# Four heads to a transfer: one decode step of attention and MLP with its reads regrouped into 64-KB rows

## The chip, the core and the metric

The kernel runs on one NeuronCore of a Trainium2 chip. The metric is device time in microseconds (us) from the start to the end of one execution. A NeuronCore has a matrix engine (TensorE, "PE" in the profile, its weight loads "PEld"), VectorE ("DVE"), ScalarE ("ACT"), GpSimd ("POOL") and SyncE ("SP"), which here only issues transfers. Each engine runs its own instructions in order and waits for others by semaphores. Sixteen DMA engines bring data from device memory (HBM) into the on-chip memory SBUF, which has 128 partitions. PE writes its results into PSUM, a smaller memory with 128 partitions and eight banks of 512 fp32 columns.

## What is computed

One token for each of two batch entries goes through attention over a cache of 4,096 keys and values in 32 heads of 128, and through an MLP; a sigmoid gate mixes the two. Everything is fp32. Cut to what matters:

```python
B, Sq, D = 2, 1, 576
H, Sk, Dh = 32, 4096, 128
F = 4608

def _A_ref(x, k_cache, v_cache, wq, wo):
    B, Sq, D = x.shape
    H, Dh = 32, 128
    q = (lambda x, *d: x.transpose(*d))((x @ wq).reshape(B, Sq, H, Dh), 0, 2, 1, 3)
    scores = jnp.einsum("bhqd,bhkd->bhqk", q, k_cache) * (Dh ** -0.5)
    p = _softmax(scores, axis=-1)
    o = jnp.einsum("bhqk,bhkd->bhqd", p, v_cache)
    return (lambda x, *d: x.transpose(*d))(o, 0, 2, 1, 3).reshape(B, Sq, H * Dh) @ wo

def _B_ref(x, w1, b1, w2, b2):
    h = jnp.einsum("bsd,df->bsf", x, w1) + b1
    h = _gelu(h)
    return jnp.einsum("bsf,fd->bsd", h, w2) + b2

x = A_x
g = _sigmoid((x * gate_w).sum(-1, keepdims=True))
a = _A_ref(x, A_k_cache, A_v_cache, A_wq, A_wo)
b = _B_ref(x, B_w1, B_b1, B_w2, B_b2)
return g * a + (1 - g) * b
```

K and V hold 134.2 MB each; wq and wo 9.4 MB each, w1 and w2 10.6 MB each. Each byte is used once for the one token of its batch entry (the weights once for both).

## The kernel before

The unit of work is one head of one batch entry, 64 units in all. A unit's K is 4,096 rows of 128 numbers, 2 MB. `load_head` (L94) brings it in with one transfer, 32 consecutive rows to a partition, so that each partition receives one run of 16 KB; V the same way. Weights come in by `load_w` (L83: wq and w1 in pieces of 128 rows, 16 or 18 KB to a partition, and a last piece of 64 rows cut in two halves), `load_w2` (L100: eight pieces, 11.5 or 9.2 KB to a partition, the last one cut further) and `load_wo` (L139: sixteen pieces, two runs of 2.3 KB to a partition).

**Order of the transfers.** All large transfers are issued by SP. A list (`seq`, L114 to 121) fixes the order: wq, w1, K0, K1, then V(i) and K(i+2) in turn, then w2. They share nine buffers of 18 KB to a partition (`SLOTS`, L59), taken in rotation; a transfer waits until the last reader of its buffer is done. wo has two buffers of its own and is issued at every fourth unit, between the others. x, the gate's weights, b1 (as 512 runs of 36 bytes) and b2 are issued by ACT at the start (L147 to 150). The order of the instructions on every engine is the order of the program (`manual_schedule`, L75).

**Start.** x is transposed on PE (L181), the gate is computed (L188 to 196), `proj` (L199) multiplies x with wq: four column groups of PE work side by side, each with 32 columns of weights (x for both batch entries and zeros) and 512 columns of wq. The result, one row of q per batch entry and quarter, is copied to `qrow`. `q_unit` (L224) spreads four heads' q over all 128 partitions with one more matmul and a copy by ScalarE (L232), since VectorE needs q on every partition. Then b2 goes into the accumulator `acc` (L253) and `proj` multiplies x with w1. `mlp_t` (L270) transposes the MLP's hidden row in 36 pieces, three at each of twelve units, and `mlp_gelu` (L276) makes the activations.

**A unit**, in four stages that lie one pass of the loop (L368) apart:

- scores: VectorE multiplies K in place with q, first 12 of the 32 rows of each partition (`mul_a`, L300), then 20 (`mul_b`, L307). The sums over 128 numbers: the first 12 rows by ScalarE, one activation with an accumulator for each (L302), the other 20 by one VectorE reduction (L311); then the largest score of each partition (L315);
- softmax: PE transposes the 128 maxima (L319), VectorE takes the largest (L323), PE spreads it (L325), ScalarE takes the exponentials and their sums (L331);
- AV: eight matmuls per unit, each with four rows of V to a partition (512 columns), in four column groups in turn (L338), and a copy by ScalarE (L346). In the trace each fp32 matmul is two matmul instructions, each with its weight load;
- `combine` and `norm`: five matmuls pick the useful parts out of the AV result and add them over the partitions (L352, L355); VectorE divides by the sum (L360, L363). After every second unit `wo_mm` multiplies the head's result for both batch entries with its 128 rows of wo into `acc` (L246).

**End.** When the last unit is done, `mlp_out` (L288) multiplies the MLP's activations with w2 into `acc`; VectorE and ScalarE copy half of `acc` each (L415, L416), and SP and ACT write the result (L419).

Of the kernel before, what the change touches and what calls it, by code (L numbers as in the profile page):

```python
# [13 lines left out]

ACT_ROWS = 12
# [3 lines left out]
def kernel(  # L19
# [18 lines left out]
    N = B * H  # L38
    R = SK // P
    RB = 512 // DH  # L40
    NT = R // RB
    NX = D // P
    HALF = D - NX * P
    assert HALF * 2 == P
    NG = 4
    WQ = H * DH
    QG = WQ // NG
    HU = 512 // DH
    FG = F // NG
    FR = FG // P  # L50
    FB = 3
    FC = FG // FB
    NF = F // P
    HO = 2
    UO = HO * B
    NC = 4
    DO = D // NC
    SCALE = float(DH) ** -0.5
    SLOTS = 9  # L59
    W2A = 5  # L60
    PL = 120

    cp = ctx.enter_context(tc.tile_pool(name="cp", bufs=1))
    bp_ = ctx.enter_context(tc.tile_pool(name="bp_", bufs=SLOTS))
    wp2 = ctx.enter_context(tc.tile_pool(name="wp2", bufs=2))
    qp = ctx.enter_context(tc.tile_pool(name="qp", bufs=4))
    sp = ctx.enter_context(tc.tile_pool(name="sp", bufs=4))
    ep = ctx.enter_context(tc.tile_pool(name="ep", bufs=2))
    ps_acc = ctx.enter_context(tc.tile_pool(name="ps_acc", bufs=1, space=bass.MemoryType.PSUM))
    ps_av = ctx.enter_context(tc.tile_pool(name="ps_av", bufs=2, space=bass.MemoryType.PSUM))  # L70
    ps_big = ctx.enter_context(tc.tile_pool(name="ps_big", bufs=1, space=bass.MemoryType.PSUM))
    ps_sm = ctx.enter_context(tc.tile_pool(name="ps_sm", bufs=4, space=bass.MemoryType.PSUM))


    ctx.enter_context(tc.manual_schedule())  # L75


    kt, vt, wqt, wot, w1t, w2t = {}, {}, {}, {}, {}, {}

    def slot(name, n):  # L80
        return bp_.tile([P, FG * NG], F32, tag="slot", name=name)[:, :n]

    def load_w(w, c, name):  # L83

        n = w.shape[1]
        if c < NX:
            t = slot(f"{name}{c}", n)
            nc.sync.dma_start(t, w[c * P:(c + 1) * P])
        else:
            t = slot(f"{name}{c}", n // 2)  # L90
            nc.sync.dma_start(t, w[NX * P:].rearrange("q (e n) -> (q e) n", e=2))
        return t

    def load_head(src, i, name):  # L94

        t = slot(f"{name}{i}", R * DH)
        nc.sync.dma_start(t, src[i % B, i // B].rearrange("(p r) d -> p (r d)", p=P))
        return t.rearrange("p (r d) -> p r d", d=DH)

    def load_w2(g, part):  # L100
        lo, hi = (0, W2A) if part == 0 else (W2A, FR)
        t = slot(f"w2_{g}_{part}", (hi - lo) * D)
        src = w2[g * FG:(g + 1) * FG].rearrange("(p r) n -> p (r n)", r=FR)
        if (g, part) == (NG - 1, 1):

            m = hi - 1
            nc.sync.dma_start(t[:, :(m - lo) * D], src[:, lo * D:m * D])
            for a, z in ((0, PL), (PL, P)):
                nc.sync.dma_start(t[a:z, (m - lo) * D:], src[a:z, m * D:hi * D])
        else:  # L110
            nc.sync.dma_start(t, src[:, lo * D:hi * D])
        return t.rearrange("p (r n) -> p r n", n=D)

    seq = [("wq", c) for c in range(NX + 1)] + [("w1", c) for c in range(NX + 1)]  # L114
    seq += [("k", 0), ("k", 1)]
    for i in range(N):
        seq.append(("v", i))
        if i + 2 < N:
            seq.append(("k", i + 2))
    seq += [("w2", (g, part)) for g in range(NG) for part in range(2)]  # L120
    seq = seq[::-1]

    def load(n=1):
        for _ in range(n):
            if not seq:
                return
            kind, i = seq.pop()
            if kind == "wq":
                wqt[i] = load_w(wq, i, "wq")
            elif kind == "w1":  # L130
                w1t[i] = load_w(w1, i, "w1_")
            elif kind == "k":
                kt[i] = load_head(k_cache, i, "k")
            elif kind == "v":
                vt[i] = load_head(v_cache, i, "v")
            else:
                w2t[i] = load_w2(*i)

    def load_wo(g):  # L139
        t = wp2.tile([P, HO, D], F32, tag="wo", name=f"wo{g}")  # L140
        nc.sync.dma_start(t, wo[g * HO * P:(g + 1) * HO * P].rearrange("(c p) n -> p c n", p=P))
        return t

    xg = cp.tile([B + 1, D], F32, name="xg")
    b1T = cp.tile([P, NG, FR], F32, name="b1T")
    b2r = cp.tile([B, D], F32, tag="row", name="b2r")
    nc.scalar.dma_start(xg[:B], x.rearrange("b s d -> (b s) d"))  # L147
    nc.scalar.dma_start(xg[B:B + 1], gate_w[None, :])
    nc.scalar.dma_start(b1T, b1.rearrange("(g p r) -> p g r", p=P, r=FR))
    nc.scalar.dma_start(b2r[:1], b2[None, :])  # L150
    load(SLOTS)


    ident = cp.tile([P, P], F32, name="ident")
    make_identity(nc, ident)
    ones = cp.tile([P, P], F32, name="ones")
    nc.vector.memset(ones, 1.0)
    srow = cp.tile([1, P], F32, name="srow")
    nc.vector.memset(srow, SCALE)
    NPB = 4  # L160
    pt = []
    for j in range(NPB):
        t = cp.tile([P, 2 * R], F32, name=f"p{j}")
        nc.vector.memset(t, 0.0)
        pt.append(t)

    sel = cp.tile([P, RB], F32, name="sel")
    nc.vector.tensor_copy(sel, ident[:, 0:RB])
    for j in range(1, 4):
        nc.vector.tensor_add(sel, sel, ident[:, 32 * j:32 * j + RB])  # L170

    xe = cp.tile([B + 1, 2, P], F32, name="xe")
    nc.vector.memset(xe, 0.0)
    for e in range(2):
        nc.vector.tensor_copy(xe[:, e, e::2], xg[:, NX * P:])
    xps = ps_sm.tile([P, NX + 2, 4], F32, tag="sm", name="xps")
    for c in range(NX + 2):
        src = xg[:, c * P:(c + 1) * P] if c < NX else xe[:, c - NX]  # L180
        nc.tensor.transpose(xps[:, c, :B + 1], src, ident[:B + 1, :B + 1])  # L181
    xT = cp.tile([P, NX + 2, 32], F32, name="xT")
    nc.vector.memset(xT, 0.0)
    nc.vector.tensor_copy(xT[:, :, :B], xps[:, :, :B])
    gT = cp.tile([P, NX + 2], F32, name="gT")
    nc.vector.tensor_copy(gT, xps[:, :, B])

    zps = ps_sm.tile([P, B], F32, tag="sm", name="zps")  # L188
    for c in range(NX + 1):
        nc.tensor.matmul(zps, gT[:, c:c + 1].to_broadcast([P, P]), xT[:, c, :B], start=(c == 0), stop=(c == NX))  # L190
    gb = cp.tile([P, B], F32, name="gb")
    g1 = cp.tile([P, B], F32, name="g1")
# [6 lines left out]
    def proj(c, t, banks, width):  # L199
        for m, ps in enumerate(banks):  # L200
            for j in range(NG):
                o = (j * len(banks) + m) * width
                lhs = xT[:, c]
                if c == NX:
                    half = NG * len(banks) * width // 2
                    lhs = xT[:, NX + o // half]
                    o %= half
                nc.tensor.matmul(
                    ps[32 * j:32 * j + 32, :width], lhs, t[:, o:o + width], start=(c == 0), stop=(c == NX),
                    skip_group_check=True,  # L210
                )
# [24 lines left out]
    for b in range(B):  # L236
        q_unit(0, b)
# [210 lines left out]
```

## Time and profile before

| | |
|---|---|
| median of 3 runs | 743.46 us (743.27 to 743.82) |
| span of the profiled execution | 742.0 us, so that 1.5 us of the median lies around the span |
| DMA, mean over the span | 417 GB/s, 309.10 MB in 26,121 packets |
| PE, PEld | 470.7 and 228.8 us busy |
| DVE | 513.7 us busy |
| ACT | 311.7 us busy |
| mean granted clock of PE | 0.636 of full speed |

How to read it. The profile is one execution, recorded by the hardware. Its first part gives each engine's busy time, the second cuts the span into 40 equal slices (a digit is a busy share in tenths, "DMA" the mean share of the sixteen DMA engines, GB/s what they moved). The third lists the DMA queues: q1 is SP's, q10 is ACT's, q8 and q14 carry the engines' own instructions; a packet is one contiguous run moved by one engine. The chain of waits is followed back from the last instruction: at each step to what released it. In the groups by line, "x64" is a count, then come busy time and the mean duration of one in nanoseconds, then the idle time of the engine just before, with what ended it. The table of windows lists for a stretch its length, the busy time and count of PE, PEld, DVE, ACT and POOL, PE's granted clock, the DMA share and GB/s. In the timeline a row has start, duration, engine, line and operation, and in brackets the idle time before it. "SPq" is SP's instruction queue.

### The profile page before, as it was taken

The page shows a single profiled execution, that of the slowest core. Times are in us where ns is not written, and L with a number is a line of the kernel's source. Part 1 is how long each engine was busy: PE and PEld are TensorE (multiplying, and loading weights), DVE is VectorE, ACT ScalarE, POOL GpSimd, SP SyncE. Part 2 cuts the span into 40 slices and gives each one's busy share as a digit, 9 for nine tenths or more (in the row PEclk, how much of TensorE's full clock was granted, in tenths as well). Part 3 has the DMA queues.
Part 4 walks back from the last instruction along what each step waited for, and adds up shares of the span by engine and source line. Part 5 has one row for each costly group of instructions (what it writes and reads, how often), then busy time and mean ns, then how long its engine had stood idle before and what let it go on. Part 6 is the DMA issues. An engine that isn't in the chain of part 4 may idle for free.

```text
span 742.0 us, 8332 instructions
## 1 busy us (share of the span) xinstructions
PE 470.7 (63%) x2728; PEld 228.8 (31%) x2728; DVE 513.7 (69%) x477; ACT 311.7 (42%) x1817; POOL 0.7 (0%) x6
## 2 busy tenths in 40 slices
PE   4660869687766667667575665656555765566675
PEld 2110435354423323223231232222222333232343
DVE  1009869777887777886878867787778877777820
ACT  0104545444554445544445534454444544354410
POOL 0000000000000000000000000000000000000000
PEclk9985566657555655565656656666665665555568
DMA  9999999999999999999999999999999999999992
GB/s 368 427 427 423 429 424 430 422 430 423 426 427 427 423 430 425 425 426 427 426 426 427 424 427 425 428 427 426 427 426 428 424 427 425 429 422 428 424 422 108
DMA packets 26121, 309.10 MB, mean 417 GB/s; under 512 B 3155, under 2 KB 3163, under 8 KB 7519
## 3 DMA queue, kind: packets, MB, share of 16 engines
q1 hardware_dynamic: 25535, 308.56, 98.5%
q8 instruction: 21, 0.34, 0.2%
q14 instruction: 21, 0.17, 0.1%
q10 hardware_dynamic: 544, 0.03, 0.1%
HBM read 308.57 MB, written 0.00 MB: 416 GB/s over the span
## 4 chain that ended last, share of the span: by engine, by line
DMA 85%; PE 9%; DVE 5%; issue 0%; ACTq 0%; ACT 0%; DVEq 0%; SPq 0%
DMA k<-in_A_k_cache_dram 76%; PE av L338 8%; DMA w<-in_B_w_dram 6%; DVE k L300 4%; DMA b1T<-in_B_b_dram 3%; PE bp L325 1%; DVE nm L323 0%; DVE s L311 0%; DVE k L307 0%; PE acc L246 0%; PE op L352 0%; ACTq L147 0%; PE op L355 0%; PE mt L319 0%; DVE osb L415 0%
## 5 line engine op out<-in xcount | busy, mean ns | idle before, releaser
L302 ACT ACTIVATE k<-k 128x128 f32<-128x128 f32 x768 | 225.6, 295 | 297.6 <-DVE k L300 297.6
L300 DVE TENSOR_TENSOR k<-k,q 128x1536 f32<-128x1536 f32 x64 | 112.5, 1758 | 173.6 <-DMA k<-in_A_k_cache_dram 173.6
L338 PE MATMUL av<-v,p 128*32 128x512 f32 x1024 | 226.5, 1035 | 0.0
L311 DVE TENSOR_REDUCE s<-k 128x20 f32<-128x2560 f32 x64 | 179.8, 2810 | 0.1
L307 DVE TENSOR_TENSOR k<-k,q 128x2560 f32<-128x2560 f32 x64 | 179.4, 2803 | 0.0
L302 ACT ACTIVATION_READ_ACCUMULATOR k<-k 128x1 f32 x768 | 143.7, 187 | 0.0
L325 PE MATMUL bp<-nm,srow 1*128 1x1 f32 x128 | 36.9, 355 | 133.8 <-DVE nm L323 133.8
L352 PEld LDWEIGHTS op<-sel,avs 128*128 128x128 f32 x512 | 87.5, 258 | 3.7 <-issue 2.1
L352 PE MATMUL op<-sel,avs 128*128 128x1 f32 x512 | 84.7, 287 | 0.7 <-ACT avs L346 0.7
L319 PE MATMUL mt<-ident,m 128*1 128x128 f32 x64 | 20.4, 319 | 90.6 <-DVE m L315 90.1
L325 PEld LDWEIGHTS bp<-nm,srow 1*128 1x128 f32 x128 | 31.5, 304 | 139.4 <-DVE nm L323 137.5
L338 PEld LDWEIGHTS av<-v,p 128*32 128x32 f32 x1024 | 38.1, 159 | 84.2 <-issue 83.2
L319 PEld LDWEIGHTS mt<-ident,m 128*1 128x1 f32 x64 | 5.3, 83 | 143.1 <-DVE m L315 138.2
L346 ACT COPY avs<-av 128x512 f32<-128x512 f32 x64 | 37.4, 585 | 26.5 <-PE av L338 26.1
L355 PE MATMUL op<-rs,ones 128*128 128x1 f32 x128 | 31.2, 313 | 0.0
L355 PEld LDWEIGHTS op<-rs,ones 128*128 128x128 f32 x128 | 28.9, 278 | 0.0
L246 PE MATMUL acc<-wo,oT 128*2 128x144 f32 x256 | 18.4, 371 | 15.6 <-DMA wo<-in_A_wo_dram 15.0
L246 PEld LDWEIGHTS acc<-wo,oT 128*2 128x2 f32 x256 | 5.9, 91 | 61.7 <-issue 51.2
L227 PE MATMUL qb<-qrow,ident 128*128 128x512 f32 x32 | 23.6, 828 | 0.7 <-ACT q L232 0.7
L272 PEld LDWEIGHTS htp<-ident,hrow 128*128 128x128 f32 x72 | 18.5, 332 | 11.8 <-issue 11.6
L331 ACT ACTIVATE p<-s,bs 128x32 f32<-128x32 f32 x64 | 20.6, 321 | 2.1
L232 ACT COPY q<-qb 128x512 f32<-128x512 f32 x16 | 9.4, 585 | 26.6 <-PE qb L227 26.6
(57 smaller groups left out, 173.8 us busy)
## 6 DMA issues: line engine op xcount, KB each, us to landing
k<-in_A_k_cache_dram SPq DMA_DIRECT2D x64, 2048.0 KB, 35.1
v<-in_A_v_cache_dram SPq DMA_DIRECT2D x64, 2048.0 KB, 36.4
w<-in_B_w_dram SPq DMA_DIRECT2D x4, 2304.0 KB, 19.4
wo<-in_A_wo_dram SPq DMA_DIRECT2D x16, 576.0 KB, 36.4
wq<-in_A_wq_dram SPq DMA_DIRECT2D x4, 2048.0 KB, 14.7
w<-in_B_w_dram SPq DMA_DIRECT2D x4, 1440.0 KB, 37.0
w<-in_B_w_dram SPq DMA_DIRECT2D x4, 1152.0 KB, 26.0
wq<-in_A_wq_dram SPq DMA_DIRECT2D x1, 1024.0 KB
```

The costliest lines, as they stand in the source:

```text
L227: nc.tensor.matmul(ps, ident[:, 32 * j + b:32 * j + b + 1].to_broadcast([P, P]), qrow[:, m * 512:(m + 1) * 512], start=True, stop=True,)
L246: nc.tensor.matmul(acc[32 * s:32 * s + m], lhsT, rhs[:, s * DO:(s + 1) * DO], start=start, stop=stop, skip_group_check=True)
L300: nc.vector.tensor_mul(kt[i][:, :a], kt[i][:, :a], q.to_broadcast([P, a, DH]))
L302: nc.scalar.activation(kt[i][:, r], kt[i][:, r], AF.Copy, accum_out=st[i][:, r:r + 1])
L307: nc.vector.tensor_mul(kt[i][:, a:], kt[i][:, a:], q.to_broadcast([P, R - a, DH]))
L311: nc.vector.tensor_reduce(st[i][:, a:], kt[i][:, a:], AX.X, ALU.add)
L319: nc.tensor.transpose(mt[i], mx[i], ident)
L325: nc.tensor.matmul(bias[i], srow, nm, start=True, stop=True)
L338: nc.tensor.matmul(ps[32 * j:32 * j + 32], p[:, RB * t:RB * t + 32], vt[i][:, RB * t:RB * (t + 1)].rearrange("p r d -> p (r d)"), start=(t ...
L346: nc.scalar.copy(avs[i], ps)
L352: nc.tensor.matmul(ops[i][:, 0:1], avs[i][:, r * DH:(r + 1) * DH], sel[:, r:r + 1], start=(r == 0), stop=(r == RB - 1))
L355: nc.tensor.matmul(ops[i][:, 1:2], ones, rs[i], start=True, stop=True)
```

## The change

Nothing of what is computed changes. The unit is now a *quad*: four heads of one batch entry, 16 quads.

- **K and V.** `load_quad` reads the 8 MB of four heads with one transfer: 32 partitions to a head, 128 consecutive rows to a partition, one run of 64 KB each. Three slots of 64 KB to a partition take the place of the nine buffers: K alternates between slots 0 and 1, V has slot 2 alone (the last V goes to slot 0).
- **Order.** In pass i: scores of quad i; K(i+2) is issued, which waits for the sums over K(i) in the same slot; `combine` of quad i-1; AV of quad i; V(i+1) is issued, which waits for AV of quad i.
- **q.** The projection itself spreads q: for each batch entry and head its weights are one column of x, repeated 32 times, so that the result stands on the 32 partitions of that head. It stays in four PSUM banks, from where VectorE reads it. `q_unit` goes, and the scale is put into x (`xq`).
- **Scores.** VectorE alone multiplies and sums: one multiply and one reduction over all 128 rows of a partition. The maximum per 32 partitions is found by VectorE's 32 x 32 transpose, without PE. ScalarE takes four exponentials per quad, one for each head.
- **AV and combine.** 32 matmuls per quad. `combine` adds into one PSUM bank `oall` for all quads, four matmuls and one for the sums; division and transposition are done once at the end.
- **wq and w1** are read with four (or three) consecutive rows to a partition, 32 KB and 54 KB runs, into the slots that K and V take later. **w2 and wo** are read at the end, in runs of up to 63 KB, into slots that K and V have left: 28 of w2's 36 rows per partition after AV of quad 14, 28 of wo's 32 after the sums of quad 15, the rest after AV of quad 15. b1 is 128 runs of 144 bytes.
- **The MLP's** hidden row is transposed by VectorE (in slot 2) ahead of the first quad, and its product with b2 stands ahead of the q projection on PE. At the end two accumulators are added by PE, into whose bank the last four rows of wo go directly.

The new code, cut to its core:

```python
slots = [sb(f"slot{i}", P, SLOT) for i in range(3)]
...
    def load_quad(src, i, s):
        g, b = divmod(i, B)
        dma(slots[s], src[b, g * HQ:(g + 1) * HQ].rearrange("h (p r) d -> (h p) (r d)", p=HP))
...
    for u in range(2):
        nc.tensor.matmul(acc, g1z[:, u], b2r[:, u * DW:(u + 1) * DW], start=(u == 0), stop=False, skip_group_check=True)

    def q_mm(c, t, m, last):
        v = t.rearrange("p (g h d) -> p g h d", h=HQ, d=DH)
        for b in range(B):
            for h in range(HQ):
                nc.tensor.matmul(
                    qps[b][m][HP * h:HP * (h + 1)], xq[:, c, b:b + 1].to_broadcast([P, HP]), v[:, :, h],
                    start=(c == 0), stop=last, skip_group_check=True,
                )

    for c in range(NX):
        for m in range(2):
            o = c * WQ + m * WQ // 2
            q_mm(c, slots[0][:, o:o + WQ // 2], m, False)
    for e in range(2):
        q_mm(NX + e, wqh, e, True)
...
    def qk(i, s):
        g, b = divmod(i, B)
        k = slots[s].rearrange("p (r d) -> p r d", d=DH)
        q = qps[b][g // 4][:, (g % 4) * DH:(g % 4 + 1) * DH]
        nc.vector.tensor_mul(k, k, q.unsqueeze(1).to_broadcast([P, R, DH]))
        nc.vector.tensor_reduce(stt[i % 2], k, AX.X, ALU.add)
        nc.vector.tensor_reduce(mxt[i % 2], stt[i % 2], AX.X, ALU.max)
        nc.vector.transpose(mtt[i % 2], mxt[i % 2].to_broadcast([P, 32]))
        nc.vector.tensor_reduce(nmt[i % 2], mtt[i % 2], AX.X, ALU.max, negate=True)
        for h in range(HQ):
            a = slice(HP * h, HP * (h + 1))
            nc.scalar.activation(
                pt[i % 2][a, h:R * HQ:HQ], stt[i % 2][a], AF.Exp, bias=nmt[i % 2][a], accum_out=rst[i % 2][a]
            )

    def av(i, s):
        v = slots[s]
        for t in range(NT):
            j = t % 4
            nc.tensor.matmul(
                avp[i % 2][32 * j:32 * j + 32], pt[i % 2][:, 16 * t:16 * t + 32], v[:, 512 * t:512 * (t + 1)],
                start=(t < 4), stop=(t >= NT - 4),
            )
        nc.scalar.copy(avt[i % 2], avp[i % 2])
...
    def acc_row(name, r, last=False):
        lhs = (hg if name == "w2" else oT)[:, r]
        s = nset[0] % 2
        nset[0] += 1
        for u in range(2):
            nc.tensor.matmul(
                acc[64 * s + 32 * u:64 * s + 32 * u + B], lhs, wrow[name, r][:, u * DW:(u + 1) * DW],
                start=False, stop=last, skip_group_check=True,
            )

    load_quad(k_cache, 0, 0)
    load_quad(k_cache, 1, 1)
    load_quad(v_cache, 0, 2)
    N1 = NQ - 1
    for i in range(NQ):
        qk(i, i % 2)
        if i < NQ - 2:
            load_quad(k_cache, i + 2, i % 2)
        elif i == NQ - 2:
            load_quad(v_cache, N1, i % 2)
        else:
            load_rows("wo", 0, WA // 2, N1 % 2, 0)
            load_rows("wo", WA // 2, WA, N1 % 2, WA // 2)
        if i > 0:
            combine(i - 1)
        av(i, 2 if i < N1 else (NQ - 2) % 2)
        if i < NQ - 2:
            load_quad(v_cache, i + 1, 2)
        elif i == NQ - 2:
            load_rows("w2", 0, WA, 2, 0)
    load_rows("w2", WA, FR, 0, 0)
    load_rows("wo", WA, OR - 1, 0, FR - WA)
    load_rows("wo", OR - 1, OR, 0, FR - WA + OR - 1 - WA)
    combine(N1)
...
    for r in range(WA):
        acc_row("w2", r)
    for r in range(WA):
        acc_row("wo", r)
    for r in range(WA, FR):
        acc_row("w2", r, last=r >= FR - 2)
...
    accs = avt[1][:, :DW]
    nc.vector.tensor_copy(accs, acc)
    fin = qps[0][0][:, :DO]
    for v in range(4):
        nc.tensor.matmul(
            fin[32 * v:32 * v + B], fsel[:, v // 2], accs[:, (v % 2) * DO:(v % 2 + 1) * DO],
            start=True, stop=False, skip_group_check=True,
        )
    for r in range(WA, OR):
        for v in range(4):
            nc.tensor.matmul(
                fin[32 * v:32 * v + B], oT[:, r], wrow["wo", r][:, v * DO:(v + 1) * DO],
                start=False, stop=r == OR - 1, skip_group_check=True,
            )
```

(HQ is 4, HP 32, R 128, NT 32, NX 4, WA 28, FR 36, OR 32, DW 288, DO 144.)

More of the change, by code (lines that the diff above doesn't have):

```diff
@@ L13 @@
 P = 128
-ACT_ROWS = 12
 @with_exitstack
@@ L80, in slot @@
[L80 to L98, printed above, removed]
@@ L114 @@
[L114 to L137, printed above, removed]
@@ L139, in load_wo, with sb @@
[L139 to L146, printed above, removed]
+    pp = ctx.enter_context(tc.tile_pool(name="pp", bufs=1, space=bass.MemoryType.PSUM))
+    ctx.enter_context(tc.manual_schedule())
+    def sb(name, *shape):
+        return cp.tile(list(shape), F32, tag=name, name=name)
@@ L409 @@
[L409 to L416 removed]
+                oall[a, b * DH:(b + 1) * DH], sel[:, gp, rr], avt[i % 2][:, rr * DH:(rr + 1) * DH],
+                start=first and rr == 0, stop=last and rr == 3, skip_group_check=True,
+            )
+        nc.tensor.matmul(
+            oall[a, B * DH + b:B * DH + b + 1], hsel[:, gp], rst[i % 2], start=False, stop=last, skip_group_check=True
+        )
@@ L417 @@
+    osb = avt[0][:, :DO]
+    nc.vector.tensor_copy(osb, fin)
     for b in range(B):
```

395 lines of the change are left out of this document (157 added, 238 removed).

## The prediction

> **What bounds the kernel now.** I read the page first: busy shares, the forty slices, the queues and the chain.
>
> ```profile
> span 742.0 us, 8332 instructions
> PE 470.7 (63%) x2728; PEld 228.8 (31%) x2728; DVE 513.7 (69%) x477; ACT 311.7 (42%) x1817; POOL 0.7 (0%) x6
> DMA  9999999999999999999999999999999999999992
> GB/s 368 427 427 423 429 424 430 422 430 423 426 427 427 423 430 425 425 426 427 426 426 427 424 427 425 428 427 426 427 426 428 424 427 425 429 422 428 424 422 108
> q1 hardware_dynamic: 25535, 308.56, 98.5%
> q8 instruction: 21, 0.34, 0.2%
> q14 instruction: 21, 0.17, 0.1%
> q10 hardware_dynamic: 544, 0.03, 0.1%
> DMA 85%; PE 9%; DVE 5%; issue 0%; ACTq 0%; ACT 0%; DVEq 0%; SPq 0%
> ```
>
> The DMA engines are full from the first slice to the last but one, no compute engine passes 69%, and 85% of the chain is DMA. The bytes must all be read once, before and after (308.56 MB). So three things can move the time: the rate of a full queue, holes in it, and the two ends. The table of windows shows the rate and the end:
>
> ```profile
> 0.00:5.00 5.00, 0.00 (x0) 0.00 (x0) 1.42 (x11) 1.28 (x1) 0.70 (x6) 1.00 0.65 207
> 24.00:47.00 23.00, 13.90 (x116) 3.85 (x108) 0.00 (x0) 2.34 (x4) 0.00 (x0) 0.93 1.01 429
> 47.00:66.00 19.00, 6.04 (x49) 1.80 (x49) 9.08 (x5) 5.05 (x27) 0.00 (x0) 0.73 1.01 430
> 120.00:660.00 540.00, 345.30 (x1811) 167.76 (x1803) 417.21 (x374) 249.84 (x1470) 0.00 (x0) 0.61 1.01 426
> 700.00:710.00 10.00, 6.79 (x31) 3.71 (x31) 7.71 (x10) 4.66 (x28) 0.00 (x0) 0.50 1.01 415
> 708.00:721.00 13.00, 10.67 (x78) 5.75 (x82) 1.39 (x7) 1.74 (x5) 0.00 (x0) 0.75 1.02 428
> 724.00:728.00 4.00, 3.65 (x110) 2.76 (x104) 0.00 (x0) 0.00 (x0) 0.00 (x0) 0.91 0.79 286
> 728.00:732.00 4.00, 2.25 (x70) 1.42 (x60) 0.00 (x0) 0.00 (x0) 0.00 (x0) 1.00 0.36 129
> 732.00:736.00 4.00, 1.70 (x44) 1.20 (x40) 0.00 (x0) 0.00 (x0) 0.00 (x0) 0.87 0.06 26
> ```
>
> The last two columns are DMA share and GB/s. In 732 to 736 the share is 0.06, one engine of sixteen: fifteen are done and one still works. The chain of waits shows the same lag in the middle:
>
> ```profile
> 122.09 1.76 DVE k L300
> ...
> 165.67 3.23 PE av L338 x16
> ...
> 330.42 3.62 PE av L338 x16
> ...
> 658.57 1.76 DVE k L300
> ...
> 736.44 2.12 PE acc L246 x32
> ```
>
> From 122.09 to 658.57 lie 13 groups of four heads, 41.27 us each. A group reads four K, four V and one wo piece, 17.37 MB, which at the mean 426 GB/s takes 40.77 us. A landing counts when its last sixteenth is in, so the slowest engine falls 0.50 us behind the mean in each group, about 8 us over sixteen: the tail just seen. The end of the kernel is the end of that one engine.
>
> **The change: fewer, longer rows.** By the code, the kernel before reads 22,912 rows on q1: K and V 16,384 of 16 KB, wo 4,096 of 2.3 KB, w2 1,152, wq and w1 1,280 (the rest of the 25,535 packets are completions). The changed one reads 5,632: K and V 4,096 of 64 KB, wq and w1 768, w2 256, wo 512. If a row stays one packet, 17,280 fixed costs go. What is one worth? Group of four at 426 GB/s: 1,280 rows, 40.77 us. The same bytes at the 429 of window 24 to 47 (w1, 18-KB rows, 942 of them): 40.48 us. So 338 rows cost 0.29 us on 16 engines, 13.5 ns each; the rounding of both rates gives 9 to 18. From above, the 544 small packets of q10 hold 0.05 to 0.15% of 16 x 742 us, 11 to 33 ns each with their bytes. I take 10.5 ns, near the low end, since the 23 us window is short and q10 packets carry bytes too. Gain: 17,280 x 10.5 / 16 = 11.3 us (bounds 9.7 and 19.4).
>
> The Trainium skill, DMA: Bandwidth & Descriptors, section Where 436 GB/s comes from, gives the ports a ceiling of 435.2 GB/s. By it the bytes need 709.0 us against 724.3 at 426, so at most 15.3 us can go; no run here shows the ceiling itself.
>
> **Instruction fetches.** q8 and q14 carry 0.34 and 0.17 MB, two to one, and PE with its weight loads has 5,456 of 8,332 instructions, also two to one; so I take q8 for PE's stream, on one engine. A packet of 0.34/21 MB takes that engine 0.61 us at a sixteenth of 428 GB/s, 12.7 us in all: enough for the 8 us lag. After, counting two instructions per fp32 matmul as the trace does: AV 1,024, q 160, w1 120, combine 160, w2 and wo rows 256, end and start 60; 1,780, with loads 3,560, or 14 packets. Seven fewer are worth 4.3 us at most and nothing if the lag has another cause. I take 3.5.
>
> **What must stay hidden.** One 8.39 MB transfer takes 19.35 us at the new rate (16 KB at 428 GB/s is 612 ns on an engine, 602 without the fixed cost, so 64 KB takes 2,418 ns: 433.5 GB/s); a K and a V take 38.7 us. Two waits can open a hole. K(i+2) waits for VectorE's sum over K(i), and the single V slot makes V(i+1) wait for all of av(i), with only K(i+2) in the queue meanwhile. On SP both waits are in order, V's wait holding up K(i+3), which isn't due before.
>
> ```profile
> L338 PE MATMUL av<-v,p 128*32 128x512 f32 x1024 | 226.5, 1035 | 0.0
> L338 PEld LDWEIGHTS av<-v,p 128*32 128x32 f32 x1024 | 38.1, 159 | 84.2 <-issue 83.2
> L300 DVE TENSOR_TENSOR k<-k,q 128x1536 f32<-128x1536 f32 x64 | 112.5, 1758 | 173.6 <-DMA k<-in_A_k_cache_dram 173.6
> L307 DVE TENSOR_TENSOR k<-k,q 128x2560 f32<-128x2560 f32 x64 | 179.4, 2803 | 0.0
> L311 DVE TENSOR_REDUCE s<-k 128x20 f32<-128x2560 f32 x64 | 179.8, 2810 | 0.1
> L315 DVE TENSOR_REDUCE m<-s 128x1 f32<-128x32 f32 x64 | 11.9, 186 | 6.6
> L278 DVE TENSOR_TENSOR hb<-htp,b1T 128x72 f32<-128x72 f32 x1 | 0.2, 223 | 0.0
> L280 DVE TENSOR_TENSOR gt<-hb 128x72 f32<-128x72 f32 x1 | 0.2, 232 | 0.0
> ```
>
> VectorE: a multiply costs (2803 - 1758)/1024 = 1.02 ns an element, so 16,384 take 1758 + 14,848 x 1.02 = 16.9 us; the reduce, at (2810 - 186)/2528 = 1.04 ns, 17.2 us; maximum, transpose, maximum 0.7 us. With q read from PSUM: L278, which has a PSUM operand, is no dearer than L280. Sum 34.8 us of 38.7: hidden, 3.9 us to spare, and behind it K(i+2) isn't due until V(i) has landed. The four exponentials per quad on ScalarE come over 20 us ahead of V. The ScalarE sums, PE's maxima and q's copies that go, and the fewer combines, lay beside the transfers: they return nothing.
>
> PE: av(i) is 64 instructions. Sixteen take 3.62 us where the granted clock is down (0.50 in window 700 to 710), so 14.5 us at most. The timeline has the same shape in the start:
>
> ```profile
> 18.68 3.32 PE L208 MATMUL qps<-wq,xT 128*32 128x512 f32 x16 [2.57 <-DMA wq<-in_A_wq_dram]
> 23.68 1.92 PE L208 MATMUL qps<-wq,xT 128*32 128x512 f32 x16 [1.68 <-DMA wq<-in_A_wq_dram]
> 0.74 2.44 SPq L88 DMA_DIRECT2D wq<-in_A_wq_dram  x4
> ```
>
> The second set took 1.92 us, with the clock above 0.9 there (0.93 in window 24 to 47): 7.7 us for 64. An issue needs 1.8 us at most to start moving bytes (207 GB/s in the first 5 us means full rate from 2.58; issue at 0.74). So V(i+1) is asked for in time with 19.35 - 14.5 - 1.8 = 3.0 us to spare at the worst clock. The forecast has no hole here; what one would cost is rival two.
>
> **The start.** From the chain of waits, the groups by line and, for the end below, the timeline:
>
> ```profile
> 1.61 22.41 DMA b1T<-in_B_b_dram
> ```
>
> ```profile
> L208 PE MATMUL hps<-w,xT 128*32 128x384 f32 x120 | 13.5, 600 | 9.9 <-DMA w<-in_B_w_dram 9.9
> L208 PE MATMUL qps<-wq,xT 128*32 128x512 f32 x80 | 13.0, 793 | 4.8 <-DMA wq<-in_A_wq_dram 4.8
> ```
>
> ```profile
> 738.59 0.30 DVE L415 COPY osb<-acc 64x144 f32<-64x144 f32 x1 [17.80 <-PE acc L246]
> 739.22 0.62 SPq L419 DMA_DIRECT2D out_dram<-osb  x1
> ```
>
> K0 needs slot 0, free after the first 128 q instructions; ahead of it lie wq and w1, 20.05 MB, until 2.6 + 46.9 = 49.5 us. New is that b2's product stands before q on PE, and b2 queues behind b1T, which took 22.41 us in 512 pieces; now 128 pieces, each waiting behind 32-KB instead of 16-KB rows, so about half. From 16 us, 128 x 0.163 (13.0 us for 80) ends at 37; from 24 at the cold 3.32/16 it ends at 51, and K0 is 3 us late. I take zero, up to 3. K1 waits for 32 more q instructions and 72 of w1 (13.5 us for 120): about 50, due at 69. V0 waits for the rest of w1 and the hidden row's few us on ScalarE and VectorE: about 60, due at 88.
>
> **The end.** Now 5.6 us pass from 736.44 to 742.0. After, behind w2's last rows, which land 2.8 us before the last 1.2 MB, PE has 32 instructions of 288 columns (about 3 us; the chain's last row gives 66 ns for 144), VectorE a copy of 288 columns (0.45; L415 took 0.30 for 144), PE 8 small ones (0.5) and 32 for wo (2.1 as in that last row), then copy and output as now (0.3 and 2.8), and gaps 0.2: 9.3 less 2.8 is 6.5. So +0.9 (bounds -1 and +3).
>
> **Sum.** 742.0 - 11.3 - 3.5 + 0.9 = 728.1 us of span. The median, 743.46, is 1.5 above the span shown; so 729.6 us.
>
> **Rivals.**
> One, the rows are cut: the longest packet in the trace of before is 18 KB (w1), so that 64 KB stays whole isn't shown. Cut at 32 KB costs 2.7 us, inside my range. Cut at 16 KB only some 3,900 packets of wo, w2 and the rest go: 2.6 us for 11.3, time 738.3. For it: nothing but that lack.
>
> Two, slower: the one V slot. If av(i) lasts over 17.5 us, every quad leaves a hole of the excess, fifteen times. PE's loads (159 ns) lie beside its matmuls now, 38.1 us busy in all against 226.5; were none hidden, 64 x (226 + 159) = 24.6 us, a hole of 7.1, and 729.6 + 106 = 836. The gain is eaten from 0.9 us of hole a quad. Against it: 14.5 us is the cold pace, and the dense run at the start went on at 0.93.
>
> Three, slower: VectorE bounds. It does from 38.7 us a quad, that is if the multiply with PSUM takes 23% longer. At half as long again, 8.5 - 3.9 = 4.6 us, fifteen times: 799. Against it L278.
>
> Four, slower: the reads collide. With 8 of the 128 rows to an engine, its share then starts 512 KB from the next, where it was 128. If K and V run at 415, the slowest ten microseconds above, instead of 433.5, 268.4 MB take 28 us longer: 757. Against it: 16-KB rows read at 430, 18-KB ones, no power of two, at 429.
> The Trainium skill, DMA: Bandwidth & Descriptors, section Latency and other measured facts, speaks for this rival: copies at a row pitch of 512 KiB ran at 207 GB/s against 214 full, and slower at larger ones. Its smallest pitch is above our 64 KB, and no row here shows the effect.
>
> Five: a late start only, 732 to 735, inside the range.
>
> **Chances.** Forecast with its bounds (724 to 735) 0.70; cut rows 0.12 (738); V slot 0.05; VectorE 0.05; collisions 0.05; nothing moves or a mishap of another kind 0.03. This kernel's measurement tells 0.2%, 1.5 us: faster than 742.0 in the first two, 0.82; same 0.03; slower 0.15. The range runs from 723 (rows worth 15 ns, all of the fetches, an end no longer than now) to 741 (cut rows and a late start).
>
> **What would show it.** Right: the queues' line falls from 25,535 to some 6,300 packets, GB/s in the middle 432 to 435, q8 near 14 packets, the tail in which one engine works shorter, DMA at 9 in every slice, VectorE idle some 4 us a quad waiting for K. Wrong: packets at 10,000 or more (cut rows), DMA slices under 9 with SP's queue waiting on av (V slot) or on the sums (VectorE), or a full queue at under 426 GB/s (collisions).

## The result, and the profile after

The changed kernel takes 725.88 us (median of 4 runs, 725.42 to 726.44) against 743.64 us (743.27 to 744.23) for the kernel before: a ratio of 0.9763, 95% interval 0.9749 to 0.9777, or 17.8 us less. The forecast was 729.6 us in a range of 723 to 741. The direction and most of the mechanism were right. The gain was 17.8 us where 13.9 were forecast, and one of its terms had been put down to the wrong engine's instructions.

From the page of the changed kernel: the span, the busy shares, the DMA slices and rates, the queues and the chain, as shown for the kernel before.

```profile
span 723.5 us, 4047 instructions
PE 218.5 (30%) x1780; PEld 76.9 (11%) x1780; DVE 572.6 (79%) x127; ACT 45.7 (6%) x150; POOL 0.7 (0%) x6
DMA  9999999999999999999999999999999999999995
q1 hardware_dynamic: 6344, 308.55, 98.8%
q8 instruction: 14, 0.23, 0.1%
q10 hardware_dynamic: 160, 0.03, 0.0%
q14 instruction: 3, 0.02, 0.0%
DVE 53%; DMA 42%; PE 4%; issue 0%; ACTq 0%; DVEq 0%; SPq 0%
```

The DMA engines are full in every slice but the last, as before. q1 has 6,344 packets for the same bytes: a 64-KB row did stay one packet. q8 has the 14 packets forecast. Two things in these lines were not in the forecast: q14 falls from 21 packets to 3, and the chain names VectorE with 53%. The windows of the changed kernel (length, busy time of PE, PEld, DVE, ACT and POOL, PE clock, DMA share, GB/s):

```profile
120.00:660.00 540.00, 139.69 (x1019) 48.32 (x1021) 504.03 (x72) 36.61 (x125) 0.00 (x0) 0.63 1.00 433
712.00:716.00 4.00, 4.00 (x48) 1.27 (x40) 0.00 (x0) 0.00 (x0) 0.00 (x0) 0.63 0.86 359
716.00:720.00 4.00, 3.34 (x76) 1.62 (x70) 0.46 (x1) 0.00 (x0) 0.00 (x0) 1.00 0.23 91
720.00:724.00 4.00, 0.20 (x8) 0.00 (x0) 0.31 (x1) 0.00 (x0) 0.00 (x0) 0.72 0.00 1
```

A full queue moves 433 GB/s in place of 426; 433.5 was forecast for K and V. The ceiling of 435.2 GB/s that the Trainium skill gives for the ports (DMA: Bandwidth & Descriptors, Where 436 GB/s comes from) stands just above this, so the rate agrees with it. The tail, in which the share falls to one engine in sixteen, has shrunk: before, the last engine worked alone from 732 to 736, some 8 us after the first ones ran out; here the share goes from 0.86 to 0.00 within 8 us. The trace's semaphore events say it directly, one event for each sixteenth of a transfer: in the kernel before the last sixteenth lands 2.2 us behind the first at 0.2 ms and 11.3 us behind in the last large transfer, 5.6 us after the next to last; in the changed kernel it lands 2.4 and 3.3 us behind the first.

The costliest groups of the changed kernel, by line:

```profile
L232 DVE TENSOR_TENSOR slot<-slot,q 128x16384 f32<-128x16384 f32 x16 | 275.5, 17218 | 45.5 <-DMA slot<-in_A_k_cache_dram 45.5
L247 PE MATMUL av<-slot,p 128*32 128x512 f32 x1024 | 145.6, 732 | 454.7 <-DMA slot<-in_A_v_cache_dram 454.7
L233 DVE TENSOR_REDUCE st<-slot 128x128 f32<-128x16384 f32 x16 | 275.5, 17220 | 1.5
```

VectorE's multiply and reduction take 17.2 us each (16.9 and 17.2 were forecast), 35.2 us a quad with the small ones. It waits for K 45.5 us in all, 12.5 of them ahead of K0 and some 3.4 us a quad from the eighth on, and PE waits for V. Nothing that the transfers need comes late, in spite of VectorE's share of the chain (see the run `dve_2p5`).

### The profile page after: what moved, and what is told of

It reads as the page before. It is cut to its first block, busy times and chain, and to the rows that moved or that the text cites. A ratio compares the mean times of both kernels' runs of the same rounds, so it can differ in the third digit from the quotient of the medians.

```text
span 723.5 us, 4047 instructions
## 1 busy us (share of the span) xinstructions
PE 218.5 (30%) x1780; PEld 76.9 (11%) x1780; DVE 572.6 (79%) x127; ACT 45.7 (6%) x150; POOL 0.7 (0%) x6
## 3 DMA queue, kind: packets, MB, share of 16 engines
q1 hardware_dynamic: 6344, 308.55, 98.8%
## 4 chain that ended last, share of the span: by engine, by line
DVE 53%; DMA 42%; PE 4%; issue 0%; ACTq 0%; DVEq 0%; SPq 0%
DMA slot<-in_A_k_cache_dram 34%; DVE st L233 26%; DVE slot L232 26%; DMA slot<-in_A_wo_dram 6%; DMA slot<-in_B_b_dram 3%; PE q L172 2%; PE misc L286 1%; PE misc L165 0%; DVE mx L234 0%; DVE mt L235 0%; PE q L353 0%; DVE nm L236 0%; ACTq L70 0%; DVE avs L344 0%; PE q L347 0%
## 5 line engine op out<-in xcount | busy, mean ns | idle before, releaser
L232 DVE TENSOR_TENSOR slot<-slot,q 128x16384 f32<-128x16384 f32 x16 | 275.5, 17218 | 45.5 <-DMA slot<-in_A_k_cache_dram 45.5
L247 PE MATMUL av<-slot,p 128*32 128x512 f32 x1024 | 145.6, 732 | 454.7 <-DMA slot<-in_A_v_cache_dram 454.7
L233 DVE TENSOR_REDUCE st<-slot 128x128 f32<-128x16384 f32 x16 | 275.5, 17220 | 1.5
L247 PEld LDWEIGHTS av<-slot,p 128*32 128x32 f32 x1024 | 40.1, 132 | 547.7 <-issue 547.7
L239 ACT ACTIVATE p<-st,nm 32x128 f32<-32x128 f32 x64 | 33.0, 516 | 185.7 <-DVE nm L236 184.4
L251 ACT COPY avs<-av 128x512 f32<-128x512 f32 x16 | 9.4, 585 | 396.7 <-PE av L247 396.7
L260 PE MATMUL oall<-avs,sel 128*32 128x128 f32 x128 | 17.0, 276 | 12.3 <-ACT avs L251 12.3
L172 PE MATMUL q<-slot,xq 128*32 128x512 f32 x160 | 18.7, 630 | 0.0
L260 PEld LDWEIGHTS oall<-avs,sel 128*32 128x32 f32 x128 | 12.7, 109 | 26.8 <-ACT avs L251 26.8
L239 ACT ACTIVATION_READ_ACCUMULATOR p<-st,nm 32x1 f32 x64 | 12.5, 196 | 0.0
L286 PEld LDWEIGHTS misc<-slot,hg 128*2 128x2 f32 x144 | 3.7, 92 | 13.9 <-DMA slot<-in_B_w_dram 7.9
```

What stands on the lines that cost most here:

```text
L172: nc.tensor.matmul(qps[b][m][HP * h:HP * (h + 1)], xq[:, c, b:b + 1].to_broadcast([P, HP]), v[:, :, h], start=(c == 0), stop=last, skip_gr ...
L232: nc.vector.tensor_mul(k, k, q.unsqueeze(1).to_broadcast([P, R, DH]))
L233: nc.vector.tensor_reduce(stt[i % 2], k, AX.X, ALU.add)
L239: nc.scalar.activation(pt[i % 2][a, h:R * HQ:HQ], stt[i % 2][a], AF.Exp, bias=nmt[i % 2][a], accum_out=rst[i % 2][a])
L247: nc.tensor.matmul(avp[i % 2][32 * j:32 * j + 32], pt[i % 2][:, 16 * t:16 * t + 32], v[:, 512 * t:512 * (t + 1)], start=(t < 4), stop=(t > ...
L251: nc.scalar.copy(avt[i % 2], avp[i % 2])
```

## The experiments

Three theories of the lag's fall were set against each other, since it is worth more than the forecast gave it. A: the engine that ends last is the one that fetches ScalarE's instructions (q14), and the change takes 1,667 of ScalarE's 1,817 instructions away, 1,536 of them the sums of L302. B, the prediction's: it is the one that fetches PE's (q8). C: one engine has dearer rows, so that its lag fell with the number of rows. From the page of the kernel before, these 1,536:

```profile
L302 ACT ACTIVATE k<-k 128x128 f32<-128x128 f32 x768 | 225.6, 295 | 297.6 <-DVE k L300 297.6
L302 ACT ACTIVATION_READ_ACCUMULATOR k<-k 128x1 f32 x768 | 143.7, 187 | 0.0
```

All runs, each compared with the kernel before on its own chip (there it took 743.4 to 743.7 us):

| run | median us | ratio to before (95%) | q1, q8, q14 packets |
|---|---|---|---|
| changed kernel | 725.88 | 0.9763 (0.9749 to 0.9777) | 6,344, 14, 3 |
| act_pad | 730.87 | 0.9830 (0.9815 to 0.9844) | 6,344, 14, 15 |
| pe_pad | 729.67 | 0.9812 (0.9797 to 0.9826) | 6,344, 29, 3 |
| before_dve | 738.33 | 0.9928 (0.9914 to 0.9943) | 25,535, 21, 8 |
| rows16 | 733.12 | 0.9861 (0.9845 to 0.9878) | 20,168, 14, 4 |
| rows_short | 728.98 | 0.9807 (0.9793 to 0.9820) | 11,384, 14, 3 |
| av3 | 810.72, one run | | 6,344, 30, 3 |
| dve_2p5 | 727.64 | 0.9786 (0.9770 to 0.9803) | 6,344, 14, 3 |
| dve_8 | 799.08, one run | | 6,344, 14, 3 |
| tail | 727.41 | 0.9785 (0.9770 to 0.9799) | 6,488, 14, 3 |
| tail2 | 726.82 | 0.9781 (0.9768 to 0.9795) | 7,640, 14, 3 |

**ScalarE's instructions back, without their work (act_pad).**

```diff
+    pad = sb("pad", P, 1)
...
         nc.scalar.copy(avt[i % 2], avp[i % 2])
+        for _ in range(96):
+            nc.scalar.copy(pad, ident[:, :1])
```

> The changed kernel with 96 one-column ScalarE copies added behind each quad's AV copy, 1,536 in all; ScalarE stays idle most of the time and nobody waits for them. Theory A (the engine that ends last is the one that fetches ScalarE's instructions, q14, 8 KB at a time, and each fetch costs it 0.69 us): q14 goes from 3 packets to about 15, the last engine falls 7 to 8 us behind again, time 731 to 734. Theory B (mine before: PE's fetches on q8 are the lag): 726, no change. Theory C (the lag is a dearer row on one engine, so it fell with the number of rows): 726, no change.

730.87 us, 5.0 more than the changed kernel. From its page and its windows at the end:

```profile
q8 instruction: 14, 0.23, 0.1%
q14 instruction: 15, 0.12, 0.0%
```

```profile
712.00:716.00 4.00, 0.00 (x0) 0.00 (x0) 0.00 (x0) 3.44 (x18) 0.00 (x0) 0.92 0.90 375
716.00:720.00 4.00, 3.81 (x44) 1.34 (x48) 0.00 (x0) 3.43 (x19) 0.00 (x0) 0.65 0.23 96
720.00:724.00 4.00, 3.15 (x52) 0.93 (x40) 0.12 (x1) 1.54 (x9) 0.00 (x0) 1.00 0.06 23
```

The bytes, the rows and PE's instructions are those of the changed kernel, and fifteen engines run out when they did there (0.90 and 0.23 against 0.86 and 0.23). But in 720 to 724 one engine still works, share 0.06, as in the tail of the kernel before. In the landings the last sixteenth is 8.9 us behind. So 12 more packets on q14, 8 KB and 128 instructions each, hold one engine back, and the kernel ends when it does. The copies' own running is not what costs: in 120 to 660 the queue moves 433 GB/s as in the changed kernel, and from the last landing to the end of the span pass 4.9 us in both. B and C gave nothing here, so neither accounts for this lag. The 7 to 8 us of the expectation were too many: the other engines are 2.9 us behind the first themselves, and only what exceeds that counts.

**One part of the change alone, in the kernel before (before_dve).** `ACT_ROWS` is 0, the first multiply and the ScalarE sums go:

```diff
-ACT_ROWS = 12
+ACT_ROWS = 0
...
-        nc.vector.tensor_mul(kt[i][:, :a], kt[i][:, :a], q.to_broadcast([P, a, DH]))
-        for r in range(a):
-            nc.scalar.activation(kt[i][:, r], kt[i][:, r], AF.Copy, accum_out=st[i][:, r:r + 1])
```

> The kernel before with one part of the change alone: VectorE does all row sums (the 768 ScalarE sums and their 768 reads go; one multiply and one reduction of 32 rows a unit). Theory A: q14 falls from 21 packets to about 9, the last engine's lag from 11 us to about 4, time 736 to 738, with the same 25,500 packets on q1. Theories B and C: the same PE instructions and rows, time 743.6. A rival of its own: VectorE at about 9.7 us a unit against 10.3 us of transfers may come to bound it, then slower than 743.6.

738.33 us, 5.3 less than the kernel before, where 736 to 738 was expected. From its page and its windows:

```profile
q1 hardware_dynamic: 25535, 308.56, 99.2%
q8 instruction: 21, 0.34, 0.2%
q14 instruction: 8, 0.07, 0.0%
```

```profile
724.00:728.00 4.00, 1.77 (x56) 1.11 (x45) 0.00 (x0) 0.00 (x0) 0.00 (x0) 1.00 0.79 293
728.00:732.00 4.00, 2.50 (x60) 1.65 (x64) 0.00 (x0) 0.00 (x0) 0.00 (x0) 0.83 0.29 99
732.00:736.00 4.00, 1.01 (x20) 0.30 (x8) 0.30 (x1) 0.27 (x1) 0.00 (x0) 0.50 0.00 1
```

q1 and q8 stand where they stood in the kernel before, to the packet. Only q14 falls, from 21 to 8. The windows answer: the share is 0.79 in 724 to 728 in both kernels, so fifteen engines run out at the same time, and in 732 to 736 it is 0.00 where it was 0.06. The last sixteenth of the last large transfer lands 5.8 us behind the first in place of 11.3, and 0.1 us after the next to last. The same 5 us are taken off one kernel here and were put onto the other by act_pad. ScalarE was never late in the kernel before; what its 1,536 instructions cost was the reading of them, through transfer engines that had nothing to spare.

**PE's instructions back (pe_pad).** This kernel leaves a part of the result out: the added matmuls begin a new sum in the accumulator's bank, at a time when it holds the product with b2 alone. The transfers stay as they are.

```diff
         nc.scalar.copy(avt[i % 2], avp[i % 2])
+        for _ in range(60):
+            nc.tensor.matmul(misc[:2, 400:401], ident[:, :2], ident[:, :1], start=True, stop=True, skip_group_check=True)
```

> The changed kernel with 60 one-column matmuls added behind each quad's AV, 3,840 more PE instructions with their weight loads; PE has the time (about 10 us of 39 a quad). Theory A: q8 goes from 14 packets to about 29, spread over engines, time 726 to 728. Theory B: 15 more fetches of 0.6 us on one engine, time 735. Theory C: 726.

729.67 us (728.35 to 730.54), 3.8 more than the changed kernel, between A's and B's figures, so A too put PE's fetches too low. From its page:

```profile
q8 instruction: 29, 0.48, 0.3%
q14 instruction: 3, 0.02, 0.0%
```

So q8 is PE's, 15 more packets of 16 KB for 3,840 more instructions, 256 to a packet. But no single engine is left behind at the end. By the landings of the last transfers, seven of the sixteen parts come 4.6 to 6.4 us behind the first and one 7.9, where none was over 3.3 behind in the changed kernel. PE's fetches are spread over several engines. One costs the kernel 3.8 / 15 = 0.25 us (0.16 to 0.31 by the runs' spread), one of ScalarE's 5.0 / 12 = 0.42. The records name a queue and not a transfer engine, so that ScalarE's packets go to one of them is read from the tail and the landings: in the kernel before, 11 of the last 15 packets on q14 are each followed by a rise of about 0.7 us in the lag of the last sixteenth, and the other 4 are not. So q14 seems to carry more than ScalarE's instructions, whose 1,817 fill 14 packets of 128 and not 21. The change takes 18 packets off it, of which before_dve accounts for 13; whose the other five were, and what they cost, was not measured.

**More rows (rows16, rows_short).** In rows16 each transfer of K and V is four, with rows of 16 KB again; in rows_short wo goes row by row and w2 in runs of four rows.

```diff
-        dma(slots[s], src[b, g * HQ:(g + 1) * HQ].rearrange("h (p r) d -> (h p) (r d)", p=HP))
+        v = src[b, g * HQ:(g + 1) * HQ].rearrange("h (p r) d -> (h p) (r d)", p=HP)
+        c = SLOT // 4
+        for j in range(4):
+            dma(slots[s][:, j * c:(j + 1) * c], v[:, j * c:(j + 1) * c])
```

> The changed kernel with each 8 MB transfer issued as four of 2 MB, each a quarter of every partition's run: 16-KB rows, 16,384 of them for K and V as in the kernel before, everything else as changed. Theory A: 12,288 more rows at 10.4 ns on 16 engines, 8.0 us, time 734, K and V at 428 GB/s in place of 433, the spread of landings still about 3 us. Theory C: 8.0 us and the old lag of 10 us back, time 741. If the row's price were the upper bound of my prediction, 18 ns: 13.8 us, 740.

```diff
-        dma(t[:, (r - lo) * D:(z - lo) * D], views[name][:, r * D:z * D])
...
+        step = 1 if name == "wo" else 4
+        for r in range(lo, hi, step):
+            z = min(r + step, hi)
+            dma(t[:, (r - lo) * D:(z - lo) * D], views[name][:, r * D:z * D])
```

> The changed kernel with w2 and wo alone in short runs, at the same places in the queue: wo in single rows of 2.3 KB (4,096 of them, as in the kernel before), w2 in runs of four rows of 9.2 KB (1,152). 4,480 rows more: at the 9.4 ns of the run with 16-KB rows 2.6 us, at 10.5 ns 2.9 us; time 728.5 to 729.

rows16 takes 733.12 us, 7.2 more than the changed kernel, and rows_short 728.98, 3.1 more. The queue and the window of the middle of rows16:

```profile
q1 hardware_dynamic: 20168, 308.55, 99.2%
```

```profile
120.00:660.00 540.00, 171.92 (x1014) 43.95 (x1018) 497.59 (x72) 36.61 (x125) 0.00 (x0) 0.64 1.01 428
```

12,288 rows more, and the full queue is down from 433 to 428 GB/s. That is 7.24 x 16 / 12,288 = 9.4 ns a row; rows_short, with 4,480 rows more, gives 3.1 x 16 / 4,480 = 11 ns. The completions of the added transfers (1,536 and 560 packets) are in both. The prediction took 10.5. The last sixteenth of rows16 lands only 3.7 us behind the first: the cost lies on all engines alike, and C falls. The changed kernel's reads, with an engine's share starting 512 KB from the next, run at 433 GB/s, so the collision of the fourth rival isn't there. Nor is the slowing by row pitch of which the Trainium skill speaks (DMA: Bandwidth & Descriptors, Latency and other measured facts) to be seen at this pitch. (That the eight rows of an engine lie next to each other is taken from the prediction; no record shows it.)

**AV three times as long (av3).** The 64 matmuls of a quad run three times over; each pass starts its sum anew.

```diff
-        for t in range(NT):
+        for t in [*range(NT)] * 3:
```

> The changed kernel with every quad's 32 AV matmuls carried out three times over, the last time standing. Rival two of the prediction puts the threshold at 17.5 us per quad (one 8 MB transfer less the time from an issue to its first bytes). AV takes 8.5 to 9.6 us in the changed kernel, so about 26 here (24 if the clock stays up): a hole of 6.5 to 9 us in the queue for each of 15 quads, 100 to 130 us, time 825 to 860, DMA slices under 9 and SP's queue waiting on av. If the one V slot had other cover, 726.

810.72 us, 84.8 more; 825 to 860 was expected, with 24 to 26 us of AV where 22.3 came. Two quads of its timeline (start, busy time, engine, line, tiles, count, and the idle time before with what ended it):

```profile
242.86 22.34 PE L247 MATMUL av<-slot,p 128*32 128x512 f32 x192 [20.26 <-DMA slot<-in_A_v_cache_dram]
...
265.25 0.33 SPq L93 DMA_DIRECT2D slot<-in_A_v_cache_dram  x1
...
287.18 22.37 PE L247 MATMUL av<-slot,p 128*32 128x512 f32 x192 [20.13 <-DMA slot<-in_A_v_cache_dram]
```

A quad lasts 44.3 us in place of 38.7. V is asked for at 265.25, as soon as AV has ended at 265.20, and the next AV begins at 287.18, 21.9 us later, where a transfer in a full queue takes 19.35. Of the 21.9 us, 1.0 pass until V's first packets start (266.21; K's packets before them have ended by 262.6), 20.5 are the transfer, and 0.5 pass from the end of its last packet to AV. Fifteen holes of 5.6 us are the 84 us. So the second rival's mechanism is real, and it begins at 22.3 - 5.6 = 16.7 us of AV, where the prediction put 17.5. AV takes 8.4 to 9.7 us in the changed kernel; 7 us are to spare.

**VectorE's slack (dve_2p5, dve_8).** A further reduction over 19 or 60 of the 128 rows of a quad, to a tile that nobody reads; the line of dve_2p5:

```diff
         nc.vector.tensor_reduce(stt[i % 2], k, AX.X, ALU.add)
+        nc.vector.tensor_reduce(pad[:, :19], k[:, :19], AX.X, ALU.add)
```

> The changed kernel with a second sum over 19 of the 128 rows of K in each quad, 2.5 us more for VectorE ahead of the next K's issue: 37.7 us a quad, still under the 38.7 of two transfers. If the transfers bound the kernel, as I hold: 726, nothing. If VectorE did, being 53% of the chain of waits: 16 x 2.5 = 40 us, 766.

> The same with 60 rows, 8.1 us: 43.3 us a quad. Then VectorE bounds, by 4.6 us a quad; K(i+2) is asked for after V(i) has landed only once the slack of the first quads (some 20 us) is used up, so 15 x 4.6 = 69 less up to 20: time 775 to 795, with VectorE at nearly 100% from K0 to the end.

dve_2p5 takes 727.64 us. Of some 39 us more VectorE work 1.8 show. VectorE does not set the pace in the changed kernel, though the chain names it for 53%: it keeps step with a full queue, and a chain followed back through it takes its busy time before the transfer's. The 1.8 us are one hole, early; the windows of dve_2p5:

```profile
104.00:108.00 4.00, 0.00 (x0) 0.00 (x0) 3.97 (x4) 0.00 (x0) 0.00 (x0) 0.50 0.61 262
108.00:112.00 4.00, 1.43 (x8) 0.40 (x12) 3.96 (x3) 2.08 (x8) 0.00 (x0) 0.50 1.16 442
```

K2 takes the place of K0, whose sum ends at 105.4 us in the changed kernel and at 107.7 here, when V0 has nearly landed: the queue runs dry for 1.4 us (352 GB/s over these 8 us, 426 in the changed kernel). The prediction counted the slack of a quad in the middle and not that of the first, which is 0 to 2 us. dve_8 takes 799.08 us. Its VectorE groups:

```profile
L233 DVE TENSOR_TENSOR slot<-slot,q 128x16384 f32<-128x16384 f32 x16 | 275.4, 17212 | 12.5 <-DMA slot<-in_A_k_cache_dram 12.5
L235 DVE TENSOR_REDUCE pad<-slot 128x60 f32<-128x7680 f32 x16 | 130.3, 8143 | 0.0
```

Of the 130.3 us, 33.0 come out of the wait for K (45.5 to 12.5). What is left of it is the wait ahead of K0: from there on VectorE never waits. The rest makes VectorE late: its last maximum ends at 761.5 us, 92.8 later than in the changed kernel. The span grows by 73.6, since in the changed kernel V15, w2 and wo still came after that maximum (54.8 us to the end, 35.6 here) and 19 us of slack lay there. I had taken this slack for larger, so the time is above the 775 to 795 that were expected. The third rival's mechanism is real too, at a price near the one it was given: 35.2 + 8.1 - 38.7 = 4.6 us too many a quad, the excess that the prediction reckoned with, for 73 us in place of its 69, and far from this kernel. That it named 799 as the time is luck: its 69 us were added to 729.6.

**Another order at the end (tail, tail2).** tail puts rows 14 to 27 of wo, in pieces of ten and four, behind the last of w2; tail2 keeps the order and loads in pieces of two rows. Both expectations take 717.9 for the last landing of the changed kernel; that is the next to last, and wo's last row lands at 718.7.

```diff
-            load_rows("wo", WA // 2, WA, N1 % 2, WA // 2)
...
     load_rows("w2", WA, FR, 0, 0)
+    WB = WA - 4
+    load_rows("wo", WA // 2, WB, N1 % 2, WA // 2)
+    load_rows("wo", WB, WA, N1 % 2, WB)
```

> The changed kernel with the last transfers in another order and piece: wo 0-13, w2 28-35, wo 14-23, wo 24-27, wo 28-31, and PE's rows in the same order, so that behind the last landings only four rows are left for the accumulator in place of 14 and 8. In the changed kernel 5.6 us pass from the last landing (717.9) to the end at 723.5, PE being 0.4 us behind. If that is PE's cold work, 1.5 to 2 us go: 724. If the end is set by the landings and the output alone, 726.

```diff
-            load_rows("wo", WA // 2, WA, N1 % 2, WA // 2)
+            for r in range(WA // 2, WA, 2):
+                load_rows("wo", r, r + 2, N1 % 2, r)
...
-    load_rows("w2", WA, FR, 0, 0)
+    for r in range(WA, FR, 2):
+        load_rows("w2", r, r + 2, 0, r - WA)
```

> The changed kernel with its last transfers in the old order but in pieces of two rows to a partition (wo 14-27 in seven, w2 28-35 in four). In the run before this one the reordered tail left PE 14 rows at 0.44 us each behind a landing at 713.2, so that PE again ended the kernel. Two rows take 1.4 us to land and 0.9 us on PE, so PE should follow the landings, and behind the last one (717.9) stand 8 small matmuls, a copy and the output, 3.8 us: 721.7 of span, 724.1 us. If the landings of the pieces cost more than that, 726.

727.41 and 726.82 us against 725.88: neither gains. From the timelines, tail first:

```profile
713.24 6.14 PE L286 MATMUL misc<-slot,oT 128*2 128x288 f32 x56 [4.74 <-DMA slot<-in_A_wo_dram]
...
719.53 0.46 DVE L348 COPY avs<-misc 128x288 f32<-128x288 f32 x1 [33.95 <-PE misc L286]
```

```profile
711.48 0.67 PE L286 MATMUL misc<-slot,oT 128*2 128x288 f32 x8 [0.76 <-DMA slot<-in_A_wo_dram]
...
712.91 1.14 PE L286 MATMUL misc<-slot,hg 128*2 128x288 f32 x8 [0.76 <-DMA slot<-in_B_w_dram]
...
719.38 2.14 PE L355 MATMUL q<-slot,oT 128*2 128x144 f32 x32
```

In tail the copy of the accumulator begins at 719.53, 1.2 us after that of the changed kernel. In tail2 PE takes its rows as they land and waits between them; the same 32 matmuls that end the changed kernel in 1.16 us then take 2.14, at a granted clock of 0.50 in 716 to 724, and its last landing is at 719.2, 0.5 us later than in the changed kernel. No version tried beats the changed kernel.

## Why the prediction came out as it did

**The rows** came as forecast. "Gain: 17,280 x 10.5 / 16 = 11.3 us": rows16 and rows_short, which bring back 12,288 and 4,480 of these rows, measure 7.2 + 3.1 = 10.3 us. (The 512 rows of wq and w1 that are left would be 0.3 us more.) A row of 64 KB is one packet, so the first rival did not come.

**The step that failed** is "so I take q8 for PE's stream, on one engine", with its price: "Seven fewer are worth 4.3 us at most", 3.5 taken. q8 is PE's, but its packets are spread, and the engine that came last is the one that fetches ScalarE's instructions, on q14. Nothing was given for them: the prediction wrote of the ScalarE sums and the rest that "they return nothing", since they lay beside the transfers. Their running did; their fetching lay in the transfer engines' way. Taking them out alone is worth 5.3 us (before_dve), putting as many back costs 5.0 (act_pad). PE's seven packets, at pe_pad's 0.25 us, are worth 1.8. Together 6.8 to 7.1 us in place of 3.5, which is most of the difference between the 17.8 us gained and the 13.9 forecast. The landings agree roughly: the lag fell from 11.3 to 3.3 us. The lag itself, "about 8 us over sixteen", was read rightly; two to one in bytes and in instructions was no proof of whose it was.

**The end** was better than the +0.9 us forecast. The timeline of the changed kernel:

```profile
710.41 5.78 PE L286 MATMUL misc<-slot,oT 128*2 128x288 f32 x56 [6.04 <-DMA slot<-in_A_wo_dram]
...
716.02 2.11 PE L286 MATMUL misc<-slot,hg 128*2 128x288 f32 x32
...
718.28 0.46 DVE L344 COPY avs<-misc 128x288 f32<-128x288 f32 x1 [32.83 <-PE misc L286]
...
719.04 1.16 PE L353 MATMUL q<-slot,oT 128*2 128x144 f32 x32
```

From w2's last rows at 716.02 to the end of the span are 7.5 us, where 9.3 were counted: 2.1 for "about 3 us" and 1.2 for 2.1, since PE comes out of the 56 instructions for wo without a pause and its granted clock is 1.00 in 716 to 720. From the last landing (718.66) to the end are 4.9 us and in the kernel before (736.40) 5.6, so 0.8 us are gained here.

**The start** shows no hole, as taken.

```profile
20.43 2.25 PE L165 MATMUL misc<-slot 1*128 1x288 f32 x4 [8.87 <-DMA slot<-in_B_b_dram]
...
38.00 11.19 SPq L93 DMA_DIRECT2D slot<-in_A_k_cache_dram  x2
```

b2's product begins at 20.43, between the two cases (16 and 24): the chain's wait for b1 and b2 fell from 22.41 to 18.28 us, not to about half. K0 is asked for at 38.00, 11 us before the 49.5 at which the prediction has it due.

**What was to stay hidden** did: VectorE 35.2 us of a quad's 38.7 (34.8 forecast), AV 8.4 to 9.7 (up to 14.5), a full queue at 433 GB/s. The second, third and fourth rivals didn't come. The forecast missed only the small slack of the first quad, which dve_2p5 found.

**The sum**: 7.2 + 3.1 for rows, 5.0 to 5.3 for ScalarE's fetches, 1.8 for PE's and 0.8 for the end are 17.9 to 18.2 against the 17.8 us measured. That it meets so closely is partly luck, since PE's price is known to about a third and the other packets of q14 have none. Against the forecast the rows fell 1.0 us short, while fetches and end gave more.

## What to carry to other kernels

Where the transfer engines are full, count all that they carry: here a row cost some 10 ns on one of sixteen engines, and the instructions of PE and ScalarE were fetched through them. An engine that is idle much of the time, as ScalarE was (42% busy), can then set the end by the number of its instructions, and the sign was a tail in which the DMA share is one sixteenth. A chain that names a compute engine for half the span does not say that it bounds when a full queue keeps the same pace: give it a little more work and see.

## What the runs showed that was not expected

- A packet on q14 is 8 KB (0.12 MB in 15), one on q8 16 KB (0.48 MB in 29). The Trainium skill, Runtime: NRT & Kernel Launch, section Terms, has instructions refilled in blocks of 16 KiB; q8 agrees, q14 does not.
- The price of a q14 packet is more than its bytes. In the landings of the kernel before, and of act_pad, most show as a step of about 0.69 us by one sixteenth; 8 KB at a sixteenth of 428 GB/s is 0.31. Why such a packet counts more than double stays open.
- From the end of an AV to the first packets of the next V pass 1.0 us in av3, of which 0.33 are the issue.
- 64 matmul instructions in one run take 8.4 to 9.7 us, sixteen at a time in the kernel before 3.2 to 3.6: the granted clock rises within a run (in the one that starts at 264.87 it is 0.50 up to 267 and 1.00 from 268), and its mean is 0.785 in av3 against 0.666 in the changed kernel.
